# Hash-bucket attention and a gated convolution: two of six transposes per head through DRAM and VectorE

## The chip, the cores and the metric

The kernel runs on one NeuronCore of one Trainium2 chip. The metric is the device time of one execution in microseconds (us); lower is better. The time given for a kernel is the median of its runs. A profile is taken of one execution; its own time is called the span.

Engines are named as in the profile: PE (TensorE), DVE (VectorE), ACT (ScalarE), POOL (GpSimd), and SP, whose queue issues nearly all DMAs here.

## What is computed

The input is attention with 4 batches of 8 heads, 768 rows of 64 numbers, followed by a gated feed-forward block of width 512. Each query and key gets a bucket of 6 sign bits, and a query sees only the keys of its own bucket:

```python
mask = q_bucket[:, :, :, None] == k_bucket[:, :, None, :]
scores = scale * np.matmul(q, k.transpose(0, 1, 3, 2))
scores = np.where(mask, scores, -1000000000.0)
attn = softmax(scores)                       # max, exp, sum + 1e-9
x = (attn @ v)  laid out as (4, 768, 512)
gate = sigmoid(causal_conv(x, conv_w))       # 5 taps, per channel
out = (gate * (x @ w_val)) @ w_out
```

Everything is in 32-bit floats. The three weights arrive as 64-bit floats and are turned into a high and a low part on the chip.

## The kernel before

A head is a unit (32 of them, `units`), and each unit has six tiles of 128 queries (`tiles`, 192 in all). The main loop runs over the slot number k; slot k works on tile k at several stages at once:

- `scores(k + 1)`: four matmuls on PE write the scores of the next tile, 128 x 768, to one of two PSUM buffers `s`. The bucket mask is folded into the matmul by 12 extra rows.
- `maxima(k)`, `factors(k)`, `shifts(k)` on DVE: row maximum `nm`, then the scale `gs` and the shift `nb`. `row_sums` and `recip` do two tiles at once, on even slots.
- `exponentials(k)` on ACT: reads `s`, writes the probabilities `p` (one of four buffers, `LAG + 1`).
- `normalise(k - 2)` on POOL: divides `p` by its row sum.
- `transposes(k - 3)` on PE: six 128 x 128 transposes of `p` into two PSUM tiles `tp` of 384 columns.
- `keep_transposed(k - 4)` on ACT: two copies from `tp` to the buffers `pt`. A head has four `pt` tiles, one for each half of its queries and each half of its keys; there are six buffers.
- `attn_v`: when the sixth tile of a head has been kept, its products with v are put in the list `avs`. They are made on odd slots, two steps a slot, 24 matmul instructions a head, two query halves side by side in one PSUM tile `av`. ACT then copies them to `x`.

Beside it, lists of generators hand out work a step at a time: `preps` (the split of the next head's q and k into high and low parts, with six DMAs between buffers), `convs` (for each pair of heads, the split of `x` into `xh` and `xl`, then the five taps of the gate `g` on POOL and DVE), `moes` (the two products with the weights, in three passes of high and low parts, with the split of the hidden tile into `hh` and `hl`, and the stores of `o`), and `weights` (two chains that load and convert the weight parts in turn, with two staging buffers).

The order of instructions on PE, ACT, DVE and POOL is the order in which the loop writes them down (`manual_schedule`); each engine works through its list strictly in that order. The order of the DMAs on SP is not: a planner sets it when the program is built, and SP then issues them strictly in that order, waiting at each until its data or its buffer is ready. The lines that the prediction steps touch are L266 (scores), L272 (maxima), L282 (shifts), L290 (exponentials), L305 (normalise), L314 (transposes), L323 (copies to `pt`), L337 (`av`), L357 and L408 (the casts to `xh` and `hh`), L368 (the gate's taps), L174 to L182 (the DMAs of `prep`) and L434 (the stores).

Of the kernel before, what the change touches and what calls it, by code (L numbers as in the profile page):

```python
# [26 lines left out]
def kernel(  # L27
# [18 lines left out]
    LAG = 3  # L46
    scale = 1.0 / float(D) ** 0.5
# [9 lines left out]
    ptp = ctx.enter_context(tc.tile_pool(name="ptp", bufs=6))  # L57
# [4 lines left out]
    wst = ctx.enter_context(tc.tile_pool(name="wst", bufs=2))  # L62
# [68 lines left out]
    def load_weights(which):  # L131
        parts = [(src[:, c, :], hl[0][:, c, :], hl[1][:, c, :])
                 for src, hl in ((w_val, wv), (w_out, wo)) for c in range(NP)]
        for src, hi, lo in parts[which::2]:
            if src.dtype == mybir.dt.int64:
                w = wst.tile([P, 512, 2], I32, name="w64")
                nc.sync.dma_start(out=w, in_=src.bitcast(I32).rearrange("p (n t) -> p n t", t=2))
            else:
                w = wst.tile([P, 512], FP32, name="w32")
                nc.sync.dma_start(out=w, in_=src)  # L140
            yield
            yield from split_weight(w, hi, lo)
# [53 lines left out]
    def bits(i):  # L196

        u = stk.tile([P, S], FP32R, name="u", bufs=2)
# [85 lines left out]
    def exponentials(k):  # L284
# [5 lines left out]
        nc.scalar.activation(out=p, in_=s[:, :, 0:HS], func=AF.Exp, bias=nb, scale=gs.pop(k), accum_out=sm[:, k % 2, 0:1])  # L290
# [15 lines left out]

    def transposes(k):
# [9 lines left out]
    def keep_transposed(k):  # L317
        i, qt = tiles[k]
        if qt % 3 == 0:
            cur["pts"].append([ptp.tile([P, 3, HS], FP32, name="pt") for _ in range(2)])  # L320
        qo = (qt % 3) * P
        for pt, tp in zip(cur["pts"][-1], tps.pop(k)):
            nc.scalar.copy(out=pt[:, :, qo:qo + P], in_=tp[:, 0:HS].rearrange("p (a b) -> p a b", b=P))  # L323
        if qt == KB - 1:
            avs.append(attn_v(i, cur["pts"]))
            cur["pts"] = []

    def attn_v(i, pts):
# [4 lines left out]
        for kb in range(KB):  # L333
            if kb:
                yield
            for s, pt in enumerate(pts):
                nc.tensor.matmul(out=av[s * D:(s + 1) * D, 0:HS], lhsT=vt[:, kb, hh * D:(hh + 1) * D], rhs=pt[kb // 3][:, kb % 3, :],  # L337
                                 start=(kb == 0), stop=(kb == KB - 1), tile_position=(0, s * D))
# [11 lines left out]

    def pair_x(b, c, x, gs, xs_):
        for o in (0, HS):
# [4 lines left out]
            nc.vector.tensor_copy(out=xh, in_=x0)  # L357
# [26 lines left out]
    def moe(b, xs_, g):  # L384
# [7 lines left out]
        def val(o, j):  # L392
# [13 lines left out]
            def split():  # L406
                hh = hp.tile([P, HS], FP32R, name="hh")
                nc.vector.tensor_copy(out=hh, in_=ht)  # L408
# [6 lines left out]
        def outp(o, tb):  # L415
            for gens in weights:
                finish(gens)
# [40 lines left out]
    raws, stacks, vts, ss, nbs, ps, tps, sums, rcs, nms, gs, cur = {}, {}, {}, {}, {}, {}, {}, {}, {}, {}, {}, {}  # L458
    avs, convs, moes, early = [], [], [], {}
# [14 lines left out]
    cur["gates"], cur["end"], cur["pts"] = 0, False, []  # L474
    N = len(tiles)
    with tc.manual_schedule(engines=ENGINES):
# [4 lines left out]
        weights = [[load_conv(), load_weights(0)], [load_weights(1)]]  # L481
# [4 lines left out]
        step(weights[0])  # L486
        step(weights[1])
        ahead = [early_bits()]
        turn = 0
        for k in range(N + LAG + 1):  # L490
            if 0 <= k - LAG - 1:
                keep_transposed(k - LAG - 1)
# [9 lines left out]
            if 0 <= k - 2 < N:  # L502
                normalise(k - 2)
            if k < N:
# [24 lines left out]
            if 0 <= k - LAG < N:  # L529
# [68 lines left out]
```

## Time and profile before

| | |
|---|---|
| runs | 621.98, 623.14, 624.74 us; median 623.14 |
| span of the profiled execution | 620.8 us |
| PE busy | 585.5 us, 94% |
| DVE busy | 437.6 us, 70% |
| ACT busy | 421.4 us, 68% |
| POOL busy | 395.6 us, 64% |
| DMA, all queues | 64.64 MB, mean 104 GB/s |

A line of groups of instructions reads: source line, engine, operation, tile written <- tiles read, shapes, count | busy us, mean ns of one | idle time of the engine just before them, and what ended it. A line of the timeline reads: start, duration (both us), engine, line, operation, tiles, count, and in brackets the idle time before it. A line of waits reads: who waited, for whom, us in total, times, longest. Slot times follow from counting: the n-th row maximum (L272) is that of tile n.

### The profile page before, as it was taken

To read this page: it belongs to the slowest core of one execution; us is meant where nothing else is said; L and a number is where in the kernel's file an instruction comes from. 1 tells how busy PE (TensorE), PEld (TensorE's weight loads), DVE (VectorE), ACT (ScalarE), POOL (GpSimd) and SP (SyncE) were. 2 spreads that over 40 slices of the span, in tenths; PEclk is the share of its full clock that TensorE was granted. 3 is DMA by queue.
4 is the path that set the end of the run, shared out by engine and by line. 5 is a ranking of instruction groups with operands and counts; after the bars stand their busy time and mean duration, and the time that the engine had idled before them with its cause. 6 is when DMAs were issued, how large, how long until landed. Compare 5 with 4: busy or idle time off the path is not lost.

```text
span 620.8 us, 10648 instructions
## 1 busy us (share of the span) xinstructions
PE 585.5 (94%) x3496; PEld 423.4 (68%) x3496; DVE 437.6 (70%) x1017; ACT 421.4 (68%) x881; POOL 395.6 (64%) x373
## 2 busy tenths in 40 slices
PE   5789898989999999999999999999999999999997
PEld 2655565555657777776767777777667877775895
DVE  5869798998975866668575867569665877665532
ACT  2777777778778666777787676777787766765400
POOL 3576868778766765578564777568764777544321
PEclk9799999999999999999999999999999999999999
DMA  6467666564532235243433234333422213200111
GB/s 227 123 197 199 200 167 208 157 175 118 133 83 68 70 79 142 72 108 82 122 82 107 61 80 126 84 115 82 108 70 78 67 42 91 69 18 1 51 52 51
DMA packets 29031, 64.64 MB, mean 104 GB/s; under 512 B 4937, under 2 KB 10057, under 8 KB 28977
## 3 DMA queue, kind: packets, MB, share of 16 engines
q1 hardware_dynamic: 28832, 63.93, 37.8%
q8 instruction: 28, 0.46, 0.3%
q14 instruction: 27, 0.21, 0.1%
q10 hardware_dynamic: 144, 0.03, 0.0%
HBM read 30.60 MB, written 7.86 MB: 62 GB/s over the span
## 4 chain that ended last, share of the span: by engine, by line
PE 66%; DVE 12%; ACT 12%; DMA 5%; issue 3%; POOL 2%; SPq 1%; ACTq 0%; POOLq 0%; DVEq 0%
PE av L337 17%; PE s L266 16%; PE tp L314 12%; PE m L424 8%; PE m L399 7%; ACT p L290 5%; DVE nm L272 4%; ACT pt L323 3%; ACT x L345 2%; DMA w<-in_w_val_dram 2%; DVE g L368 2%; PE tp L399 1%; PE tp L424 1%; PE s L424 1%; DMA bk<-bq 1%
## 5 line engine op out<-in xcount | busy, mean ns | idle before, releaser
L305 POOL TENSOR_SCALAR p<-p,ri 128x768 f32<-128x768 f32 x192 | 210.5, 1100 | 156.0 <-DVE nb L282 130.8
L272 DVE TENSOR_REDUCE nm<-s 128x1 f32<-128x768 f32 x192 | 182.5, 950 | 61.2 <-PE s L266 61.0
L290 ACT ACTIVATE p<-s,nb,gs 128x768 f32<-128x768 f32 x192 | 192.6, 1003 | 46.2 <-DVE nb L282 41.9
L323 ACT COPY pt<-tp 128x384 f32<-128x384 f32 x384 | 165.7, 485 | 75.3 <-PE tp L314 74.4
L314 PEld LDWEIGHTS tp<-ident,p 128*128 128x128 f32 x1152 | 130.3, 142 | 72.2 <-issue 43.6
L314 PE MATMUL tp<-ident,p 128*128 128x128 f32 x1152 | 164.4, 279 | 2.6 <-ACT pt L323 2.1
L337 PE MATMUL av<-pt,vt 128*64 128x384 f32 x768 | 144.9, 498 | 0.0
L266 PE MATMUL s<-ak,aq 76*128 76x384 f32 x384 | 118.1, 389 | 23.2 <-ACT p L290 19.7
L266 PE MATMUL s<-bk,bq 128*128 128x384 f32 x384 | 101.3, 345 | 0.4 <-DVE bq L252 0.4
L337 PEld LDWEIGHTS av<-pt,vt 128*64 128x64 f32 x768 | 47.0, 136 | 61.5 <-issue 61.4
L266 PEld LDWEIGHTS s<-ak,aq 76*128 76x128 f32 x384 | 59.2, 194 | 38.7 <-ACT p L290 34.6
L368 DVE SCALAR_TENSOR_TENSOR g<-x,cw_sb,g 128x768 f32<-128x768 f32 x64 | 79.4, 1241 | 2.2 <-POOL g L366 2.1
L266 PEld LDWEIGHTS s<-bk,bq 128*128 128x128 f32 x384 | 71.7, 194 | 0.8 <-issue 0.8
L173 POOL TENSOR_TENSOR bq<-r,aq 128x768 fp32r<-128x768 f32 x31 | 59.2, 1909 | 0.1
L410 POOL TENSOR_TENSOR hl<-ht,hh 128x384 fp32r<-128x384 f32 x32 | 32.3, 1009 | 39.5 <-DVE hh L408 39.5
L345 ACT COPY x<-av 64x384 f32<-64x384 f32 x64 | 30.4, 475 | 29.7 <-PE av L337 29.0
L282 DVE TENSOR_SCALAR nb<-nm,gs 128x1 f32<-128x1 f32 x192 | 40.4, 211 | 3.5
L399 PE MATMUL m<-xh,wv 128*128 128x384 f32 x200 | 42.7, 337 | 0.0
L358 POOL TENSOR_TENSOR xl<-x,xh 128x384 fp32r<-128x384 f32 x32 | 33.4, 1059 | 13.8 <-DVE xh L357 13.8
L290 ACT ACTIVATION_READ_ACCUMULATOR p<-s,nb,gs 128x1 f32 x192 | 39.0, 203 | 0.0
L404 DVE TENSOR_TENSOR ht<-m,g 128x384 f32<-128x384 f32 x25 | 13.9, 556 | 35.6 <-PE m L399 29.2
L424 PE MATMUL m<-wo,hh 128*128 128x512 f32 x144 | 38.1, 394 | 0.0
(86 smaller groups left out, 486.9 us busy)
## 6 DMA issues: line engine op xcount, KB each, us to landing
r<-in_qk_dram SPq DMA_DIRECT2D x32, 384.0 KB
vt<-in_v_dram SPq DMA_DIRECT2D x16, 384.0 KB
out_dram<-o SPq DMA_DIRECT2D x24, 256.0 KB
ak<-aq SPq DMA_DIRECT2D x31, 192.0 KB
bk<-aq SPq DMA_DIRECT2D x31, 192.0 KB
bk<-bq SPq DMA_DIRECT2D x31, 192.0 KB
bq<-aq SPq DMA_DIRECT2D x31, 192.0 KB
hh<-in_qk_dram SPq DMA_DIRECT2D x16, 192.0 KB
```

The source lines that it names most:

```text
L173: nc.gpsimd.tensor_tensor(out=bq, in0=r, in1=aq.bitcast(FP32), op=ALU.subtract)
L266: nc.tensor.matmul(out=s[:, hf, 0:HS], lhsT=lq[0:n, qs], rhs=rk[0:n, hf * HS:(hf + 1) * HS], start=n == M, stop=n == P)
L272: nc.vector.tensor_reduce(out=nm, in_=s[:, :, 0:HS], axis=AX.XY, op=ALU.max, negate=True)
L290: nc.scalar.activation(out=p, in_=s[:, :, 0:HS], func=AF.Exp, bias=nb, scale=gs.pop(k), accum_out=sm[:, k % 2, 0:1])
L305: nc.gpsimd.tensor_scalar(out=p, in0=p, scalar1=rcs.pop(k), scalar2=1.0, op0=ALU.mult, op1=ALU.mult)
L314: nc.tensor.transpose(out=tp[:, n * P:(n + 1) * P], in_=p[:, kb * P:(kb + 1) * P], identity=ident)
L323: nc.scalar.copy(out=pt[:, :, qo:qo + P], in_=tp[:, 0:HS].rearrange("p (a b) -> p a b", b=P))
L337: nc.tensor.matmul(out=av[s * D:(s + 1) * D, 0:HS], lhsT=vt[:, kb, hh * D:(hh + 1) * D], rhs=pt[kb // 3][:, kb % 3, :], start=(kb == 0), s ...
L345: nc.scalar.copy(out=x[hh * D:(hh + 1) * D, o:o + HS], in_=av[s * D:(s + 1) * D, 0:HS])
L368: nc.vector.scalar_tensor_tensor(out=g, in0=x[:, k:k + S], scalar=w, in1=g, op0=ALU.mult, op1=ALU.add)
L399: nc.tensor.matmul(out=acc[:, 0:HS], lhsT=wv[wi][:, c, j * P:(j + 1) * P], rhs=xs_[(c, o)][xi], start=(m == 0), stop=(m == 11))
L424: nc.tensor.matmul(out=acc, lhsT=hs[(o, j)][hi][:, tb * P:(tb + 1) * P], rhs=wo[wi][:, j, :], start=(m == 0), stop=(m == 11))
```

## The change

From tile 60 to tile 185, the first two tiles of each head (`by_blocks`) are no longer transposed on PE. Their `exponentials` write `p` in another order of columns, in blocks of 32. After `normalise`, `put_out` stores `p` to DRAM in one DMA; `take_in`, three slots later in the loop's order, reads it back in four DMAs, one for each quarter of the partitions, which move the 32 x 32 blocks to their places; `turn_blocks`, eight slots after the tile's own slot, transposes each 32 x 32 block in place with one DVE instruction.

The buffers `pt` become four whole half-heads (three query tiles by all keys), with the columns of a tile in the order query block, key tile, key within the block; the copies of `keep_transposed` write that order and `av` reads it, for all heads. `xh` and `hh` are cast by ACT, not DVE, while the slot number is from 60 to 191 (`rounded`). The weights are converted in one chain, with one staging buffer, more steps in a slot, and a wait of two slots between a load and its use. The buffer `u` of the sign bits is one, not two.

```diff
+    QB = 32
+    G = P // QB
+    FIRST, LAST = 60, B * H * KB - KB
...
-    ptp = ctx.enter_context(tc.tile_pool(name="ptp", bufs=6))
+    ptp = ctx.enter_context(tc.tile_pool(name="ptp", bufs=4))
...
-    wst = ctx.enter_context(tc.tile_pool(name="wst", bufs=2))
+    wst = ctx.enter_context(tc.tile_pool(name="wst", bufs=1))
...
+    def load_weights():
+        for src, hl in ((w_val, wv), (w_out, wo)):
+            for c in range(NP):
...
+                since = cur["k"]
+                yield
+                while cur["k"] < since + 2:
+                    yield
+                yield from split_weight(w, hl[0][:, c, :], hl[1][:, c, :])
+                since = cur["k"]
+                while cur["k"] == since:
+                    yield
...
+    def by_blocks(k):
+
+        return FIRST <= k < LAST and k % KB < 2
...
-        u = stk.tile([P, S], FP32R, name="u", bufs=2)
+        u = stk.tile([P, S], FP32R, name="u", bufs=1)
...
-        nc.scalar.activation(out=p, in_=s[:, :, 0:HS], func=AF.Exp, bias=nb, scale=gs.pop(k), accum_out=sm[:, k % 2, 0:1])
+        to, of = p, s[:, :, 0:HS]
+        if by_blocks(k):
+            to = p.rearrange("p a b -> p (a b)").rearrange("p (g a j x) -> p a j g x", g=G, a=2, x=QB)
+            of = of.rearrange("p a (j g x) -> p a j g x", g=G, x=QB)
+        nc.scalar.activation(out=to, in_=of, func=AF.Exp, bias=nb, scale=gs.pop(k), accum_out=sm[:, k % 2, 0:1])
...
+    def put_out(k):
+
+        p, _ = ps.pop(k)
+        pds[k] = dram.tile([P, S], FP32, name="pd")
+        nc.sync.dma_start(out=pds[k], in_=p)
+
+    def take_in(k):
+
+        w = place(k)
+        rows = pds.pop(k).rearrange("(i q) (g c) -> g q i c", q=QB, g=G)
+        for g in range(G):
+            nc.sync.dma_start(out=w[g * QB:(g + 1) * QB].rearrange("q i j x -> q i (j x)"), in_=rows[g])
+
+    def turn_blocks(k):
+
+        w = place(k).rearrange("p i j x -> p (i j x)")
+        nc.vector.transpose(out=w, in_=w)
+        placed(k)
+
+    def place(k):
+
+        i, qt = tiles[k]
+        at = pts.setdefault(i, {})
+        if qt // 3 not in at:
+            at[qt // 3] = ptp.tile([P, 3, G, KB, QB], FP32, name="pt")
+        return at[qt // 3][:, qt % 3]
...
-        for pt, tp in zip(cur["pts"][-1], tps.pop(k)):
-            nc.scalar.copy(out=pt[:, :, qo:qo + P], in_=tp[:, 0:HS].rearrange("p (a b) -> p a b", b=P))
...
+        for a, tp in enumerate(tps.pop(k)):
+            nc.scalar.copy(out=place(k)[:, :, 3 * a:3 * a + 3].rearrange("p i j x -> p j i x"),
+                           in_=tp[:, 0:HS].rearrange("p (j i x) -> p j i x", i=G, x=QB))
+        placed(k)
...
-                nc.tensor.matmul(out=av[s * D:(s + 1) * D, 0:HS], lhsT=vt[:, kb, hh * D:(hh + 1) * D], rhs=pt[kb // 3][:, kb % 3, :],
+                nc.tensor.matmul(out=av[s * D:(s + 1) * D, 0:HS], lhsT=vt[:, kb, hh * D:(hh + 1) * D], rhs=pt[:, :, :, kb, :],
...
+    def rounded(out, in_):
+        if FIRST <= cur["k"] < N:
+            nc.scalar.copy(out=out, in_=in_)
+        else:
+            nc.vector.tensor_copy(out=out, in_=in_)
...
                 normalise(k - 2)
+                if by_blocks(k - 2):
+                    put_out(k - 2)
...
                 exponentials(k)
+            if by_blocks(k - 8):
+                turn_blocks(k - 8)
             if k >= 60 or k % 2:
                 step(convs)
-            for _ in range((1, 0, 2, 0, 2, 2)[k % 6]):
-                step(weights[turn])
-                turn = 1 - turn
+            for _ in range((1, 1, 2, 1, 2, 2)[k % 6]):
+                step(weights)
...
                 step(avs)
+            if by_blocks(k - 5):
+                take_in(k - 5)
-            if 0 <= k - LAG < N:
+            if 0 <= k - LAG < N and not by_blocks(k - LAG):
                 transposes(k - LAG)
```

More of the change, by code (lines that the diff above doesn't have):

```diff
@@ L129, in load_conv @@
             nc.sync.dma_start(out=cw_sb, in_=conv_w)
[L131 to L142, printed above, removed]
+    def load_weights():
+        for src, hl in ((w_val, wv), (w_out, wo)):
+            for c in range(NP):
+                if src.dtype == mybir.dt.int64:
+                    w = wst.tile([P, 512, 2], I32, name="w64")
+                    nc.sync.dma_start(out=w, in_=src[:, c, :].bitcast(I32).rearrange("p (n t) -> p n t", t=2))
+                else:
+                    w = wst.tile([P, 512], FP32, name="w32")
+                    nc.sync.dma_start(out=w, in_=src[:, c, :])
+                since = cur["k"]
[6 more added lines that the diff above has]
+                    yield
     def load_raw(i):
@@ L305, in normalise, with placed @@
         nc.gpsimd.tensor_scalar(out=p, in0=p, scalar1=rcs.pop(k), scalar2=1.0, op0=ALU.mult, op1=ALU.mult)
+    def put_out(k):
[17 more added lines that the diff above has]
+        return at[qt // 3][:, qt % 3]
+    def placed(k):
+        i, _ = tiles[k]
+        done[i] = done.get(i, 0) + 1
+        if done[i] == KB:
+            avs.append(attn_v(i, pts.pop(i)))
     def transposes(k):
@@ L335, in attn_v @@
                 yield
-            for s, pt in enumerate(pts):
-                nc.tensor.matmul(out=av[s * D:(s + 1) * D, 0:HS], lhsT=vt[:, kb, hh * D:(hh + 1) * D], rhs=pt[kb // 3][:, kb % 3, :],
+            for s, pt in sorted(pts.items()):
+                nc.tensor.matmul(out=av[s * D:(s + 1) * D, 0:HS], lhsT=vt[:, kb, hh * D:(hh + 1) * D], rhs=pt[:, :, :, kb, :],
                                  start=(kb == 0), stop=(kb == KB - 1), tile_position=(0, s * D))
@@ L356, in pair_x @@
             x0 = x[:, KW - 1 + o:KW - 1 + o + HS]
-            nc.vector.tensor_copy(out=xh, in_=x0)
+            rounded(out=xh, in_=x0)
             nc.gpsimd.tensor_tensor(out=xl, in0=x0, in1=xh.bitcast(FP32), op=ALU.subtract)
@@ L407, in split @@
                 hh = hp.tile([P, HS], FP32R, name="hh")
-                nc.vector.tensor_copy(out=hh, in_=ht)
+                rounded(out=hh, in_=ht)
                 hl = hp.tile([P, HS], FP32R, name="hl")
@@ L415, in outp @@
         def outp(o, tb):
-            for gens in weights:
-                finish(gens)
+            while weights:
+                cur["k"] += 1
+                step(weights)
             acc = acc_tile()
@@ L472, in finish @@
             step(gens)
-    cur["gates"], cur["end"], cur["pts"] = 0, False, []
+    cur["gates"], cur["end"], cur["k"] = 0, False, 0
     N = len(tiles)
@@ L480 @@
         first_prep()
[L481 removed]
+        weights = [load_weights()]
         preps = [first_bits(), prep(1)]
@@ L485 @@
         step(preps)
-        step(weights[0])
-        step(weights[1])
+        step(weights)
+        weights.insert(0, load_conv())
+        step(weights)
         ahead = [early_bits()]
-        turn = 0
         for k in range(N + LAG + 1):
-            if 0 <= k - LAG - 1:
+            cur["k"] = k
+            if 0 <= k - LAG - 1 and not by_blocks(k - LAG - 1):
                 keep_transposed(k - LAG - 1)
```

10 lines of the change are left out of this document (3 added, 7 removed).

## The prediction

> **What bounds the kernel now.** I read the page's busy line first, then the busy time by stage, then TensorE's own order of time.
>
> ```profile
> span 620.8 us, 10648 instructions
> PE 585.5 (94%) x3496; PEld 423.4 (68%) x3496; DVE 437.6 (70%) x1017; ACT 421.4 (68%) x881; POOL 395.6 (64%) x373
> PE 66%; DVE 12%; ACT 12%; DMA 5%; issue 3%; POOL 2%; SPq 1%; ACTq 0%; POOLq 0%; DVEq 0%
> ...
> 100.00:150.00 50.00, 44.67 (x284) 28.27 (x284) 46.79 (x103) 37.81 (x82) 42.03 (x39) 1.00 0.61 170
> 200.00:250.00 50.00, 49.85 (x301) 37.66 (x300) 33.89 (x80) 34.46 (x75) 33.88 (x33) 1.00 0.38 98
> 350.00:400.00 50.00, 49.92 (x301) 36.96 (x300) 36.81 (x87) 34.69 (x74) 34.46 (x33) 1.00 0.36 94
> ```
>
> The last three rows are stretches of 50 us: busy time of PE, weight load, DVE, ACT and POOL, then granted clock, DMA share, GB/s. Up to about 170 us DVE (46.79 of 50) is as full as TensorE. From 200 us TensorE has no idle time (49.85, 49.92 of 50, clock 1.00) while DVE and ACT have 13 to 16 us of 50 free. The 60th tile's row maximum stands near 173 us and the 192nd's near 561 us, so every tile that the change touches lies in the part where TensorE is full. There a microsecond off TensorE is worth up to a microsecond.
>
> Busy time of matmuls is modelled, so what a transpose costs is read from start to start:
>
> ```profile
> 301.79 1.51 PE L337 MATMUL av<-pt,vt 128*64 128x384 f32 x8
> 303.23 0.88 PE L314 MATMUL tp<-ident,p 128*128 128x128 f32 x6
> 303.86 0.59 PE L266 MATMUL s<-ak,aq 76*128 76x384 f32 x2
> ...
> 305.59 0.82 PE L314 MATMUL tp<-ident,p 128*128 128x128 f32 x6
> 306.24 0.61 PE L266 MATMUL s<-ak,aq 76*128 76x384 f32 x2
> ```
>
> Six transposes hold TensorE 303.86 - 303.23 = 0.63 us and 306.24 - 305.59 = 0.65 us, so 0.64 us a tile.
>
> **The change, part by part.** A slot is one turn of the main loop, one tile. Tiles 0 and 1 of each head from tile 60 to 185 go the new way: 21 heads, 42 tiles.
>
> *Removed.* 42 x 0.64 = **26.9 us of TensorE**. On ACT 84 copies go:
>
> ```profile
> L323 ACT COPY pt<-tp 128x384 f32<-128x384 f32 x384 | 165.7, 485 | 75.3 <-PE tp L314 74.4
> L345 ACT COPY x<-av 64x384 f32<-64x384 f32 x64 | 30.4, 475 | 29.7 <-PE av L337 29.0
> L272 DVE TENSOR_REDUCE nm<-s 128x1 f32<-128x768 f32 x192 | 182.5, 950 | 61.2 <-PE s L266 61.0
> L368 DVE SCALAR_TENSOR_TENSOR g<-x,cw_sb,g 128x768 f32<-128x768 f32 x64 | 79.4, 1241 | 2.2 <-POOL g L366 2.1
> L357 DVE CAST xh<-x 128x384 fp32r<-128x384 f32 x32 | 17.7, 567 | 12.5 <-ACT x L345 10.6
> L408 DVE CAST hh<-ht 128x384 fp32r<-128x384 f32 x32 | 17.6, 550 | 0.3
> L91 ACT ACTIVATE o<-w 128x512 f32<-128x512 f32 x8 | 5.4, 675 | 3.8 <-DMA w<-in_w_val_dram 3.3 <-DMA w<-in_w_out_dram 0.5
> ```
>
> 84 x 0.485 = 40.7 us of ACT go, hidden under TensorE, so 0.
>
> *Rounding moved from DVE to ACT.* By the loop's counts I estimate 22 xh and 24 hh of 32 each. DVE loses 22 x 0.567 + 24 x 0.550 = 25.7 us; ACT gains 46 x 0.475 = 21.9 us (the copy of 384 elements beside it), less than the 40.7 it lost. Cost 0; without the removed copies it would fill 22 of the some 120 free microseconds of ACT in this part.
>
> *Added on DVE.* 42 block transposes of 128x768. No row shows one. [...] I take the 0.95 of the one-source pass over 768 elements. Total 39.9 us, net 14 on DVE over 390 us, with room.
>
> Place matters more than total. A turn is issued after the slot's shift (nb); the second of a head stands in the ninth slot after its tile 0, and that same slot starts the head's av. So the last thing av waits for is no longer an ACT copy at the slot's head, but a DVE pass behind nb:
>
> ```profile
> 203.56 0.21 DVE L282 TENSOR_SCALAR nb<-nm,gs 128x1 f32<-128x1 f32 x1
> 204.78 0.87 PE L337 MATMUL av<-pt,vt 128*64 128x384 f32 x4
> ...
> 481.06 1.27 DVE L357 CAST xh<-x 128x384 fp32r<-128x384 f32 x2
> 484.50 0.21 DVE L282 TENSOR_SCALAR nb<-nm,gs 128x1 f32<-128x1 f32 x1
> 485.05 1.51 PE L337 MATMUL av<-pt,vt 128*64 128x384 f32 x8
> ...
> 555.98 0.21 DVE L282 TENSOR_SCALAR nb<-nm,gs 128x1 f32<-128x1 f32 x1
> 556.53 0.87 PE L337 MATMUL av<-pt,vt 128*64 128x384 f32 x4
> ```
>
> These are the first, the 17th and the last of the 21 heads. nb ends at 203.77 and av starts at 204.78: a turn of 1.0 us with its hand-over just fits. In the last head nb ends at 556.19 and av starts at 556.53: TensorE would wait 0.66 us. Done so for all 21, the waits add to 12.0 us over 14 heads (7.8 in the heads with xh casts just before, such as the 17th, 4.1 in the others). Where the casts go to ACT (1.27 us off DVE in slot eight, 0.95 of turn in their place, and an hh of 0.35 to 1.16 gone too), nb comes about 0.6 us sooner, which leaves some 2.4 of the 7.8. So **+6.5 us**; ends 0 and 21 x 1.0 = 21. While TensorE waits, the next scores and the conv's gates are queued behind av.
>
> The turn also puts off the next tile's row maximum, thus its exponential and the scores two tiles on. In slots with a gate pass (1.24 us, one in three) DVE then has nb, turn, gate and maximum in line, some 3.6 us against slots of 2.5 to 3.5: **+2 us**, ends 0 and 9 (0.45 a head).
>
> *Added: the DRAM trip.* Five DMA issues a tile, 210 in all.
>
> ```profile
> q1 hardware_dynamic: 28832, 63.93, 37.8%
> SPq L182 <- PE s L266: 103.6, 23, 7.8
> SPq L434 <- ACT o L432: 45.1, 5, 34.3
> 337.19 0.46 SPq L176 DMA_DIRECT2D bk<-bq  x1
> 339.87 0.47 SPq L177 DMA_DIRECT2D bq<-aq  x1
> ```
>
> 63.93 MB took 37.8% of 620.8 us, so 272 MB a ms; 42 x 2 x 0.393 = 33.0 MB more is 121 us, which lifts the share in this part from 0.36 to about 0.67. Not a bound. SP's issues cost 210 x 0.46 = 97 us, some 4.6 us a head of 18. Landing: L177 must wait until bk<-bq has landed, so 0.197 MB takes 339.87 - 337.19 = 2.7 us from its issue; 0.197 MB more adds 0.7: **3.4 us** a leg; ends 2.7 and twice that, 5.4, with traffic doubled. The leg back may take 3.4 and three more issues (1.4): with the leg out 8.2 us after the normalisation, against six slots of 2.5 us or more before the turn. It is hidden.
>
> [...] The trace has 2.7 us for half the bytes within SBUF; no run here shows the DRAM leg.
>
> The leg out matters for another reason. Exponentials have four p buffers; tile k+4 takes the one of tile k, now free only when its leg out has landed:
>
> ```profile
> 179.88 2.55 POOL L305 TENSOR_SCALAR p<-p,ri 128x768 f32<-128x768 f32 x2 [0.52 <-DVE nb L282]
> 186.35 1.01 ACT L290 ACTIVATE p<-s,nb,gs 128x768 f32<-128x768 f32 x1
> ...
> 276.28 0.91 POOL L305 TENSOR_SCALAR p<-p,ri 128x768 f32<-128x768 f32 x1
> 278.04 0.32 SPq L182 DMA_DIRECT2D ak<-ud  x1
> 280.18 1.01 ACT L290 ACTIVATE p<-s,nb,gs 128x768 f32<-128x768 f32 x1
> ...
> 533.68 2.56 POOL L305 TENSOR_SCALAR p<-p,ri 128x768 f32<-128x768 f32 x2 [2.10 <-DVE nb L282]
> 541.61 1.01 ACT L290 ACTIVATE p<-s,nb,gs 128x768 f32<-128x768 f32 x1
> ```
>
> First, shortest and last of 42: tiles 60 and 61 are normalised by 182.43 and the exponential of 64 starts at 186.35; tile 91 by 277.19, that of 95 at 280.18 (3.0 us, the shortest); 180 and 181 by 536.24, that of 184 at 541.61. The middle value is 5.0 us. Against 3.4 plus 0.3 for the shorter slots, 7 of 42 fall short, together 2.2 us; four more where an output store stands ahead in SP's queue. **+3 us**, ends 0 and 10. What waits behind that exponential on ACT: the next copies and av's copy, and through the score buffer TensorE.
>
> *Layout.* av now reads its 384 columns as 12 runs of 32, in all 768 matmuls. No matmul of before reads in runs. ACT's copy in three runs (485) against one run (475) is 5 ns a run: ends 0 and 11 x 5 ns x 768 = 42 us. I take 0, since a run is 128 bytes long; the exponential's new runs cost ACT 42 x 22 x 5 ns = 5 us at most, under TensorE. [...]
>
> *Weights.* The same 8 parts, one staging buffer fewer. Counting the steps, the old chains end in slot 56, the new in 53, both before the first val product; a part now has three slots from its release to its use, not two. ACT's waits for these loads are 3.8 us in all: 0, ends -3.8 and +3.8. One u buffer fewer: 3 refills, a slot behind the reads; 0. Half-head buffers: a head's pair comes free two heads later, in time; 0.
>
> **Sum.** 620.8 - 26.9 + 6.5 + 2 + 3 = 605.4 us for the profiled execution. The three runs stand 1.2 to 3.9 us above its span, the median 2.3: **607.7 us**.
>
> **Rivals.**
> *The turn takes the place of the transposes.* If it is the 1.24 us row and xh's going frees nothing, av waits 12.0 + 14 x 0.29 = 16.1 us, the maxima 6: 620.8 - 26.9 + 16.1 + 6 + 3 + 2.3 = 621. For: 14 of 21 heads show less than 1.0 us of room. Against: DVE idles 61.0 us for scores.
>
> *Slower: the leg out is caught behind another DMA on SP.* SP takes its DMAs in one order, set before the run, and stood 103.6 us at L182. That one is released just before the exponential in question (278.04 against 280.18, mostly nearer). If the leg out stands behind it, the exponential of each head's first such tile comes 0.35 + 3.4 us late, of which TensorE has perhaps 1.4 us of other work: 2.3 x 21 = 48, so 620.8 - 26.9 + 11.5 + 48 + 2.3 = 656; it decides from 0.9 us a head on (18 us, more than the rest of the gain). Against: normalising comes before L182's release in every head, 0.9 us at the least. The runs of 32 at their full 42 us (650) end on this side too.
>
> *Nothing comes back.* DVE and SP stay out of the way and ACT's relief helps: 620.8 - 26.9 - 1 + 2.3 = 595.
>
> That the tiles are not taken off TensorE at all cannot be: 252 transposes are not issued.
>
> **How the numbers follow.** Forecast 0.60 (own range 600 to 614), turn in place 0.18 (614 to 622), slower 0.12, nothing back 0.10. The range 596 to 620 leaves out the slower case and half of the edges. This kernel's measurement tells about 0.5%, 3.1 us, from no change: under 620.0 is faster. Forecast, nothing back and half of the turn case: 0.79; same 0.09; slower 0.12.
>
> **What would show it.** Transposes 900, not 1152; their copies 300; a DVE group of 42 near 0.95 us; TensorE waiting at av for it some 6 us. Wrong would be: matmuls of av above 486 ns or more than 0.19 us apart; exponentials waiting for a DMA by tens of us; PE idle above 20 us between 180 and 560; DVE's turns waiting for DMA.

## The result: 12% slower

The changed kernel takes 698.31 us (median of four runs, 696.82 to 700.04) against 622.74 for the kernel before (median of four runs too): a ratio of 1.121, 95% interval 1.119 to 1.124. The forecast was 607.7 us, in a range of 596 to 620. The profiled execution has a span of 698.3 us. First its page: the span, the busy line, the granted clock in 40 slices, and the chain of waits by engine and by line.

```profile
span 698.3 us, 10550 instructions
PE 600.8 (86%) x3244; PEld 414.9 (59%) x3244; DVE 448.7 (64%) x1014; ACT 405.8 (58%) x842; POOL 384.4 (55%) x373
PEclk9889998999999999998999899898889999999999
PE 50%; DVE 17%; DMA 14%; ACT 6%; POOL 5%; SPq 4%; issue 3%; DVEq 0%; ACTq 0%; POOLq 0%
PE av L381 17%; PE s L278 12%; DMA pt<-pd 7%; PE m L475 6%; PE tp L363 6%; DVE nm L284 5%; PE m L449 4%; ACT p L306 3%; DMA bk<-bq 3%; DVE g L418 2%; POOL bq L185 2%; DVE pt L339 2%; SPq L334 2%; POOL p L321 1%; ACT pt L368 1%
```

TensorE has 252 instructions fewer, as planned, and yet is busy for 15 us more. Its share of the chain fell from 66% to 50%; the leg back (`pt<-pd`), a transfer that the prediction had called hidden, now holds 7% of it.

Where the time went is read from busy time by stretch. The bounds are the row maxima of tiles 60, 126 and 186. The columns are the stretch and its length, busy time of PE, PEld, DVE, ACT and POOL with counts, granted clock, DMA share, GB/s. Before:

```profile
0.00:172.70 172.70, 148.09 (x902) 94.94 (x904) 145.32 (x334) 122.82 (x260) 123.09 (x116) 0.98 0.60 171
172.70:367.80 195.10, 191.11 (x1163) 141.28 (x1164) 135.93 (x327) 145.03 (x303) 129.66 (x122) 1.00 0.35 90
367.80:544.20 176.40, 174.95 (x1054) 130.55 (x1053) 120.88 (x292) 129.68 (x274) 117.03 (x110) 1.00 0.33 84
544.20:620.80 76.60, 71.35 (x384) 56.67 (x382) 35.47 (x67) 23.90 (x47) 25.86 (x26) 0.99 0.09 35
```

After:

```profile
0.00:193.60 193.60, 158.52 (x902) 99.02 (x904) 148.09 (x335) 121.95 (x260) 120.30 (x117) 0.93 0.54 153
193.60:420.20 226.60, 193.46 (x1030) 134.44 (x1032) 140.41 (x324) 136.40 (x279) 124.90 (x122) 0.92 0.55 153
420.20:621.70 201.50, 177.34 (x933) 124.66 (x929) 125.34 (x292) 122.06 (x254) 113.00 (x110) 0.92 0.53 150
621.70:698.30 76.60, 71.48 (x384) 56.82 (x384) 34.81 (x65) 25.44 (x51) 26.24 (x26) 0.99 0.12 42
```

Two losses stand apart. **Up to tile 60**, where not one trip has been made, 193.6 - 172.7 = 20.9 us. **Between tiles 60 and 186**, 428.1 - 371.5 = 56.6 us. The tail is the same.

In the middle part TensorE was idle for 5.4 us of 371.5 before, and for 57.3 of 428.1 after: +51.9. Its busy time is 370.8 against 366.1, although 26.9 us of transposes are gone: some 31.6 us of its work are mere slowness, since the granted clock is 0.92 where it was 1.00. So -26.9 + 51.9 + 31.6 = 56.6. The last term can be checked: TensorE was busy for 60.5 us of this part at a clock of 0.50, which is 30.3 us of lost work. The gain was there; waiting and the halved clock each ate more than it.

The groups of the changed kernel name the wait; a row ends with the idle time before the group and its releaser.

```profile
L381 PE MATMUL av<-pt,vt 128*64 128x384 f32 x768 | 167.1, 562 | 48.6 <-DVE pt L339 44.1
L339 DVE STREAM_TRANSPOSE pt<-pt 128x768 f32<-128x768 f32 x42 | 41.1, 978 | 49.0 <-DMA pt<-pd 48.7
```

Its waits, and then those of SyncE's own queue, with total, times and longest:

```profile
DVE pt L339 <- DMA pt<-pd: 48.7, 17, 5.2
PE av L381 <- DVE pt L339: 44.1, 15, 6.2
```

```profile
SPq L188 <- POOL bq L185: 91.3, 31, 7.2
```

VectorE stands at the turn (L339) 48.7 us for the leg back, and TensorE stands at av 44.1 us for the turn.

### One late leg back, followed through

SyncE's queue near 310 us; these are issues of DMAs, several of one kind in one row.

```profile
307.77 0.34 SPq L327 DMA_DIRECT2D pd<-p  x1
308.21 1.88 SPq L334 DMA_DIRECT2D pt<-pd  x4
312.72 0.47 SPq L186 DMA_DIRECT2D ak<-aq  x1
...
314.47 0.60 SPq L334 DMA_DIRECT2D pt<-pd  x1
319.14 0.47 SPq L188 DMA_DIRECT2D bk<-bq  x1
...
321.77 0.47 SPq L189 DMA_DIRECT2D bq<-aq  x1
322.28 1.81 SPq L334 DMA_DIRECT2D pt<-pd  x3
```

At 307.77 the second tile of a head goes out, and the four quarters at 308.21 are the first tile's. The second tile's first quarter goes at 314.47, but its other three come only at 322.28. Between them stands L188, a copy of the next head's preparation, which waits for POOL's subtraction (L185), and L189 behind it. SyncE takes its DMAs in a fixed order, so three quarters that could have gone at 315 stood 7 us behind a copy for the next head, whose first row maximum comes at 333. In 19 of the 21 heads this copy stands between the second tile's leg out and the end of its leg back. Measured over all 21 heads, from the issue of the leg out to the end of the last issue of the leg back: 6.1 us for the first tile (none over 10), 17.3 us for the second (20 of 21 over 10). The row of SyncE above has L188 behind L185 for 91.3 us in all.

What it releases, and how long TensorE had stood:

```profile
324.48 0.99 ACT L306 ACTIVATE p<-s,nb,gs 128x768 f32<-128x768 f32 x1 [0.52 <-DVE nb L294]
326.27 0.98 DVE L339 STREAM_TRANSPOSE pt<-pt 128x768 f32<-128x768 f32 x1 [1.88 <-DMA pt<-pd]
327.17 0.92 DVE L284 TENSOR_REDUCE nm<-s 128x1 f32<-128x768 f32 x1
327.30 2.83 PE L381 MATMUL av<-pt,vt 128*64 128x384 f32 x8 [3.47 <-DVE pt L339]
328.69 0.99 ACT L306 ACTIVATE p<-s,nb,gs 128x768 f32<-128x768 f32 x1 [3.13 <-DVE nb L294]
330.06 1.01 PE L278 MATMUL s<-ak,aq 76*128 76x384 f32 x2
```

The turn stands ahead of the next row maximum on VectorE, so a late leg holds up not av alone but the whole softmax: nm at 327.17, its exponential at 328.69, the next scores at 330.06. TensorE is idle for 3.47 us, and then the eight matmuls of av take 2.83 us where they took 1.51 before. That is the clock:

```profile
318.60:323.80 5.20, 4.53 (x28) 2.83 (x24) 5.16 (x11) 4.77 (x11) 3.58 (x5) 1.00 0.54 155
323.80:327.30 3.50, 0.03 (x2) 0.00 (x1) 1.55 (x5) 1.24 (x3) 1.37 (x2) 0.68 0.88 315
327.30:330.80 3.50, 3.50 (x10) 1.51 (x11) 1.22 (x5) 1.08 (x2) 1.79 (x2) 0.50 0.41 114
```

A gap of 3.5 us, and the clock is granted at 0.50 in the stretch behind it.

### The profile page after: what moved, and what is told of

The parts are those of the page before. It is cut to its first block, busy times and chain, and to the rows that moved or that the text cites. A ratio compares the mean times of both kernels' runs of the same rounds, so it can differ in the third digit from the quotient of the medians.

```text
span 698.3 us, 10550 instructions
## 1 busy us (share of the span) xinstructions
PE 600.8 (86%) x3244; PEld 414.9 (59%) x3244; DVE 448.7 (64%) x1014; ACT 405.8 (58%) x842; POOL 384.4 (55%) x373
## 4 chain that ended last, share of the span: by engine, by line
PE 50%; DVE 17%; DMA 14%; ACT 6%; POOL 5%; SPq 4%; issue 3%; DVEq 0%; ACTq 0%; POOLq 0%
PE av L381 17%; PE s L278 12%; DMA pt<-pd 7%; PE m L475 6%; PE tp L363 6%; DVE nm L284 5%; PE m L449 4%; ACT p L306 3%; DMA bk<-bq 3%; DVE g L418 2%; POOL bq L185 2%; DVE pt L339 2%; SPq L334 2%; POOL p L321 1%; ACT pt L368 1%
## 5 line engine op out<-in xcount | busy, mean ns | idle before, releaser
L321 POOL TENSOR_SCALAR p<-p,ri 128x768 f32<-128x768 f32 x192 | 200.3, 1048 | 200.5 <-DVE nb L294 133.7
L381 PE MATMUL av<-pt,vt 128*64 128x384 f32 x768 | 167.1, 562 | 48.6 <-DVE pt L339 44.1
L368 ACT COPY pt<-tp 128x384 f32<-128x384 f32 x300 | 129.5, 485 | 41.5 <-PE tp L363 40.3
L278 PE MATMUL s<-ak,aq 76*128 76x384 f32 x384 | 123.1, 403 | 35.3 <-ACT p L306 31.3
L363 PEld LDWEIGHTS tp<-ident,p 128*128 128x128 f32 x900 | 103.0, 143 | 61.8 <-issue 37.6
L363 PE MATMUL tp<-ident,p 128*128 128x128 f32 x900 | 130.8, 282 | 3.2 <-ACT pt L368 2.0
L381 PEld LDWEIGHTS av<-pt,vt 128*64 128x64 f32 x768 | 51.7, 149 | 119.5 <-issue 64.4
L278 PEld LDWEIGHTS s<-ak,aq 76*128 76x128 f32 x384 | 64.0, 205 | 73.4 <-ACT p L306 61.3
L278 PE MATMUL s<-bk,bq 128*128 128x384 f32 x384 | 105.0, 356 | 0.4 <-DVE bq L264 0.4
L418 DVE SCALAR_TENSOR_TENSOR g<-x,cw_sb,g 128x768 f32<-128x768 f32 x64 | 76.4, 1194 | 2.3 <-POOL g L416 2.1
L339 DVE STREAM_TRANSPOSE pt<-pt 128x768 f32<-128x768 f32 x42 | 41.1, 978 | 49.0 <-DMA pt<-pd 48.7
L185 POOL TENSOR_TENSOR bq<-r,aq 128x768 fp32r<-128x768 f32 x31 | 58.8, 1898 | 0.1
L389 ACT COPY x<-av 64x384 f32<-64x384 f32 x64 | 30.4, 474 | 32.3 <-PE av L381 31.5
L475 PE MATMUL m<-wo,hh 128*128 128x512 f32 x144 | 38.8, 400 | 0.0
```

Of the source, the lines that this page charges most:

```text
L185: nc.gpsimd.tensor_tensor(out=bq, in0=r, in1=aq.bitcast(FP32), op=ALU.subtract)
L278: nc.tensor.matmul(out=s[:, hf, 0:HS], lhsT=lq[0:n, qs], rhs=rk[0:n, hf * HS:(hf + 1) * HS], start=n == M, stop=n == P)
L321: nc.gpsimd.tensor_scalar(out=p, in0=p, scalar1=rcs.pop(k), scalar2=1.0, op0=ALU.mult, op1=ALU.mult)
L339: nc.vector.transpose(out=w, in_=w)
L363: nc.tensor.transpose(out=tp[:, n * P:(n + 1) * P], in_=p[:, kb * P:(kb + 1) * P], identity=ident)
L368: nc.scalar.copy(out=place(k)[:, :, 3 * a:3 * a + 3].rearrange("p i j x -> p j i x"), in_=tp[:, 0:HS].rearrange("p (j i x) -> p j i x", i= ...
```

## The experiments

All times are set against the kernel before, run on the same chip (622.5 to 623.6 us). The table has the lengths of the parts in the profiled execution, from its row maxima, and for the middle part TensorE's idle time and the time at half clock. It is the measure of all that follows. Each row is one execution, and two runs of one kernel lie up to 6 us apart, so a difference of a few microseconds between two rows is not shown by them alone. "Half clock" is time at a granted clock of 0.50.

| kernel | to tile 60 | 60 to 186 | behind | PE idle, 60 to 186 | half clock, 60 to 186 |
|---|---|---|---|---|---|
| before | 172.7 | 371.5 | 76.6 | 5.4 | 0 |
| changed | 193.6 | 428.1 | 76.6 | 57.3 | 71.6 |
| e1 new weights chain alone | 194.6 | 371.7 | 76.4 | 5.7 | 0 |
| e2 changed, no trips | 196.2 | 375.0 | 76.8 | 6.4 | 0 |
| x1 changed, turn without trip | 195.2 | 373.8 | 76.7 | 20.0 | 17.1 |
| e12 first tile only | 194.1 | 370.8 | 76.7 | 13.2 | 0 |
| e15 second tile only | 196.4 | 385.6 | 76.7 | 22.5 | 6.8 |
| e14 transposes done as well | 194.3 | 430.2 | 76.6 | 47.5 | 41.0 |
| e16 leg back one slot sooner | 193.9 | 411.0 | 76.9 | 46.0 | 47.8 |
| e17 e16, p freed at once | 194.5 | 390.9 | 76.9 | 36.1 | 27.3 |
| e10 SyncE's order by hand | 203.6 | 389.3 | 76.6 | 32.3 | 23.9 |
| e18 e10, p freed at once | 203.4 | 378.7 | 76.8 | 22.2 | 23.9 |

### The two losses parted

**e1**: the kernel before with the new `load_weights` and its step pattern, and nothing else of the change.

> The kernel before with the weights' chain of the changed kernel alone (one staging buffer, two steps of one chain in a slot); all else as before. Theory W, the chain is the cause of the 21 us that the changed kernel has lost by its 60th tile (193.6 against 172.7 us): 640 to 645 us, the 60th row maximum near 193 us, DVE waiting some 15 us for the weights' step on ACT. Theory L, the new order of columns in pt or the single u buffer is the cause: 623 us, the 60th row maximum at 173 us.

644.65 us, ratio 1.035 (1.031 to 1.039). The whole early loss is the weights' chain; behind tile 60 nothing changes.

**e2**: the changed kernel without trips.

```diff
-        return FIRST <= k < LAST and k % KB < 2
+        return False
```

> The changed kernel with no tile by blocks: every tile is transposed by TensorE, and new column order, four half-heads, one u buffer, weights in one chain and rounding on ACT stay. Theory W: the loss stays before tile 60 only, 640 to 645 us, and the stretch from tile 60 to 186 takes some 372 us as before, clock 0.97 or more. If the rounding on ACT or the new order of columns cost something, that stretch is longer than 375 us.

649.28 us, 1.043 (1.038 to 1.047). Buffers, strided reads and the moved rounding together cost 375.0 - 371.5 = 3.5 us of the middle part; the trip and the turn cost 53.

**e5**: e2 with only the leg out, as a copy that nobody reads.

> The changed kernel with every tile transposed by TensorE (as in the run without the trip, 649.3 us), and the leg out alone added: the 42 tiles are also stored to DRAM, read back by no one. The computation is whole. Theory P, the leg out is what costs (the exponential four tiles on waits for the p buffer, SP's queue gets longer): 660 us or more, exponentials waiting for that DMA by 15 us or more. Theory Q, it is the leg back, or the turn: 649 to 653 us.

649.83 us, 1.043 (1.036 to 1.049): the time is e2's, and the middle part takes 376.7 us against 375.0, so 42 stores of 0.39 MB cost no more than some 2 us.

**x1**: the turn without a trip; POOL's normalise writes straight into the place, and the exchange of the blocks between partitions is left out.

> The changed kernel without the trip: POOL's normalisation of the 42 tiles writes straight into their place in the half-head, and VectorE turns them there at the same slots. The exchange of 32x32 blocks between partition quarters is left out, so these tiles hold blocks in wrong places; all other work is there, with none of the 210 DMAs. Theory Q, the DMAs are late: 649.3 - 26.9 and some 8 for the turn's own waits, 628 to 638 us, clock in the later stretch 0.98 or more. Theory D, the turn in VectorE's order ahead of the next maximum, with TensorE's clock halved by each wait, is enough by itself: 670 us or more.

644.56 us, 1.034 (1.022 to 1.047), between what its two theories gave. With no trip at all, taking 26.9 us off TensorE gains 375.0 - 373.8 = 1.2 us of the middle part. Its two executions took 647.46 us, the profiled one, and 641.65; by the medians the gain on e2 is 4.7 us. The rest is given back:

```profile
PE av L384 <- DVE pt L342: 8.5, 6, 2.3
POOL pt L322 <- PE av L384: 8.7, 5, 4.1
```

TensorE is idle for 20.0 us in place of 6.4, and 17.1 us run at half clock. Of the idle time 8.5 us are av's wait for the turn, the first row, and 10.0 us stand behind exponentials (5.3 in e2). The second row belongs to the experiment, not to the change: POOL writes into the place and must wait until the buffer is free, so part of what is given back may not be the turn's.

### Moving the wait about

Three runs tried to lift the turn's wait; in two it was found elsewhere, in the third it grew.

**e4**: the leg back issued by ACT (`nc.scalar.dma_start` in `take_in`), past SyncE's queue.

> The changed kernel with the four DMAs of the leg back issued by ACT in place of SP; the same bytes, the same slots. Theory A, they are late because they stand in SP's queue behind DMAs that wait for POOL and for the leg out: DVE's waits for them fall from 48.7 us to under 10, the stretch from tile 60 to 186 from 428 to 360 to 380 us, the whole to 640 to 655 us. Theory B, the trip itself is slow (two DRAM legs and doubled traffic): the waits stay at 40 us or more and the time within 10 us of 698.

709.71 us, 1.140 (1.131 to 1.149). VectorE's wait for the leg is nearly gone (0.7 us); but an issue of the leg back that has to wait now holds ACT, whose next copy stands behind it. What these issues waited for was not followed up, and the time is above both forecasts:

```profile
ACT pt L368 <- DMA pt<-pd: 52.3, 11, 6.8
```

**e6**: the turn ten slots behind, not eight.

> The changed kernel with the turn ten slots behind its tile in place of eight (some 6 us later); SP's queue is planned anew. Theories A and B both expect the waits of the turn, at most 5.2 us long, to go mostly: under 12 us in all, and 645 to 665 us. If the time stays near 698 the turn's wait is not what costs, but the p buffers or the late DMAs of the next head.

699.41 us, 1.123 (1.118 to 1.129). The turn waits for its leg 4.6 us in place of 48.7; now exponentials stand 35.1 us for the p buffer that a leg out still reads. The load of v waits for the later av on SyncE, and the legs out stand behind that load (2.1 us behind the normalise on average, where it was 1.1).

```profile
ACT p L306 <- DMA pd<-p: 35.1, 14, 5.1
```

```profile
SPq L166 <- PE av L381: 34.2, 9, 5.0
```

**e7**: SyncE too in written order, otherwise the changed kernel.

```diff
-    with tc.manual_schedule(engines=ENGINES):
+    with tc.manual_schedule(engines=ENGINES | {mybir.EngineType.SP}):
```

> The changed kernel with SP's DMAs, too, in the order in which the loop writes them down, not in the planner's. Theory A, the planner's order holds the leg back behind DMAs of the next head: if so, the waits of the turn for DMA fall from 48.7 us to under 15 and the time to 660 us or less. If every order holds something up because SP has one queue for all, it is 690 us or more and the waits move to other DMAs.

842.32 us, 1.351 (1.339 to 1.364), the slowest of all. The load of v is written first in a head's preparation and waits for av of two heads before, which waits for the turn, which waits for a leg back behind that load:

```profile
DVE pt L339 <- DMA pt<-pd: 169.9, 30, 8.2
```

The written order alone was no remedy; what stands ahead of the leg in it decides.

### Is it the trip, or the place on SyncE?

**e10**: SyncE in written order, with the load of v put late and the leg back four slots behind the tile, ahead of the next head's copies.

```diff
-        load_values(i)
         r = raws[i]
...
+            if by_blocks(k - 4):
+                take_in(k - 4)
+            if late and k % KB == 3:
+                load_values(late.pop(0))
...
-            if by_blocks(k - 5):
-                take_in(k - 5)
```

> The changed kernel with SyncE's queue in written order too, in which the take of a tile stands four slots behind its row maximum, behind the turn of that slot and ahead of the next head's preparation, and the load of v's tile is moved to the fourth slot of a head. Theory Q (the trip itself is short; what makes the leg back late is what stands in front of its four issues on SyncE, which the planner of the changed kernel put behind the copies of the next head's stacks): the turn's waits for a DMA fall from 48.7 us to under 15, the stretch from the 60th to the 186th row maximum falls from 428 us to about 375-390 (373.8 with the turn and no trip), the whole to about 645-660. Rival T (the trip's traffic or its own duration): the legs stay as late as before and the whole stays at 690 or above.

669.82 us, 1.076 (1.070 to 1.083): the middle part falls from 428.1 to 389.3 with the same 42 trips, and the turn no longer waits for a DMA. So most of the loss lies in the order on SyncE and not in the trip as such. The total is above the forecast, because this order costs 10 us ahead of tile 60, and because the p buffer is late in its turn:

```profile
ACT p L309 <- DMA pd<-p: 32.1, 12, 4.4
```

**e12** and **e15**: one tile of each head by blocks, `k % KB < 1` and `k % KB == 1`.

> The changed kernel with one tile of each head by blocks in place of two (21 trips in place of 42). Theory Q (the second tile's leg back is the one whose issues stand behind the next head's preparation on SyncE): the stretch from the 60th to the 186th row maximum is about 378-390 us, that is, well below the middle between none (375.0) and two (428.1). Rival T (each trip costs the same): about 400, the middle.

> The changed kernel with only the second tile of each head by blocks (the kernel before it had only the first: 370.8 us from the 60th to the 186th row maximum, against 375.0 with none and 428.1 with both). Theory Q (the second tile's leg back is the late one, because its four issues come behind the next head's preparation on SyncE): this stretch is about 410-430 us, the whole 685-700. Rival N (the cost comes with the second trip per head, whichever it is: traffic, DRAM or p buffers): about 371-380, the whole about 645.

e12: 644.28 us, 1.035 (1.030 to 1.040); e15: 659.29 us, 1.058 (1.054 to 1.062). The first tile alone gains 4.2 us over none (of 21 x 0.64 = 13.4 us of transposes taken away), a middle part of 370.8 us, below the 378 to 390 that were expected; the second alone loses 10.6. Place matters, but e15's forecast of 410 to 430 failed: alone, the second tile's leg back takes 9.4 us, not 17.3. With one trip fewer the planner orders SyncE anew: the copy `bk<-bq` stands ahead of the end of this leg in 8 of 21 heads, in the changed kernel in 19. The losses don't add (-4.2 and +10.6 against +53.1); that each trip delays the other fits this, but which of SyncE's DMAs does it was not parted.

**e16**: one number, the leg back four slots behind (`take_in(k - 4)`), SyncE's order left to its planner.

> The changed kernel with one number changed: the take stands four slots behind its row maximum in place of five, so that the second tile's four issues are given out ahead of the next head's preparation; SyncE's order is the planner's as in the changed kernel. Theory Q: the stretch from the 60th to the 186th row maximum falls from 428 us to about 375-395, the whole to about 645-665, and the turn's waits for a DMA fall well below 48.7 us. If the planner orders SyncE by something else than the place, it stays near 698.

685.29 us, 1.099 (1.095 to 1.104). The second tile's leg back is down to 8.6 us and the turn waits 1.1 us for it. But the middle part falls only to 411.0, short of the forecast of 375 to 395, and again the p buffer takes over. The third row is SyncE's own:

```profile
ACT p L306 <- DMA pd<-p: 33.5, 10, 6.3
PE s L278 <- ACT p L306: 59.1, 47, 5.7
SPq L166 <- PE av L381: 35.0, 9, 5.6
```

SyncE now stands 35.0 us at the load of v, which waits for av (4.3 us in the changed kernel), mostly with the next head's copies right behind it. e10, which puts that load late, has no such row, and TensorE stands idle for exponentials for 19.2 us of the middle part there, in e16 for 35.0. So an early leg back alone gives back 428.1 - 411.0 = 17.1 us; the other 21.7 up to e10 come with the rest of e10's order, which was not parted further.

**e17** and **e18** take that wait away from e16 and from e10: POOL normalises a tile into its place in `pt`, and the leg out reads it there, so that `p` is free at once.

```diff
+        to = place(k).rearrange("p i j x -> p (i j x)") if by_blocks(k) else p
-        nc.gpsimd.tensor_scalar(out=p, in0=p, scalar1=rcs.pop(k), ...
+        nc.gpsimd.tensor_scalar(out=to, in0=p, scalar1=rcs.pop(k), ...
```

> The changed kernel with the take four slots behind, and POOL's normalise of a tile that goes by blocks writes into its place in the buffer of transposed probabilities; the leg out reads it there, and the leg back writes it there. So the p buffer is free when POOL is done, not when the leg out has landed. Theory R (what is left of the loss once the second leg back is early, 411.0 us from the 60th to the 186th row maximum against 370.8-375.0, is the exponentials' wait for a p buffer that a leg out still reads, 33.5 us of waiting, and the halved clock behind it): this stretch is 375-390 us, the whole 645-665. Rival T (the trips' traffic or the two turns in neighbouring slots): it stays at 405-415, the whole at 680-690.

> The kernel with SyncE's queue in written order (389.3 us from the 60th to the 186th row maximum, with 32.1 us of waits of exponentials for a leg out) and the same normalise into place. Theory R: this stretch falls to about 373-382 us, that is, what the turn without any trip takes (373.8), and all of the loss behind tile 60 is found in two waits, the late leg back and the held p buffer. Rival T: it stays at 385-395.

e17: 661.24 us, 1.062 (1.043 to 1.082), the middle part 390.9, 0.9 us above what was expected: 19.4 us of waits for the leg back have returned, and SyncE stands 45.5 us at the load of v, in 8 of 9 cases with issues of a leg back right behind it. e18: 659.84 us, 1.060 (1.053 to 1.067), the middle part 378.7, within 5 us of the turn without any trip. Its two middle stretches carry a DMA share of 0.62 and 0.63, more than the 0.55 and 0.53 of the changed kernel, in less time:

```profile
203.40:406.00 202.60, 188.29 (x1030) 130.53 (x1032) 149.40 (x324) 136.49 (x279) 128.36 (x122) 0.96 0.62 170
406.00:582.10 176.10, 168.19 (x933) 119.41 (x930) 133.56 (x293) 122.26 (x254) 116.82 (x110) 0.98 0.63 174
```

So the middle loss is parted in two steps: 428.1 - 389.3 = 38.8 us go with the order on SyncE (17.1 of them by e16's earlier leg back alone), then 389.3 - 378.7 = 10.6 with p buffers held by legs out. What is left, 7.2 us above the kernel before, is more than e2 and x1 leave without any trip (3.5 and 2.3), but by less than two runs of one kernel can differ. Traffic is not what cost: e18 has the same 42 trips. The gain has not come back with this. The forecast for the middle part was 371.5 - 15.4 = 356.1 us, and most of the 22.6 us that e18 lacks are lacking in x1 too, which has the turn and no trip.

### Does TensorE still set the pace?

**e14**: the changed kernel with the transposes of the 42 tiles done as well, their results read by nobody.

> The changed kernel with TensorE's transposes of the 42 tiles done as well, their results read by nobody (27 us of TensorE's time put back, no copies). Theory I (TensorE is no longer what sets the pace in the changed kernel: its waits and the halved clock behind them are): the whole stays within about 10 us of 698, with TensorE idle for less and the granted clock above 0.93. Rival P (TensorE's own work still sets the pace): 698 + 27 = 725 us.

704.00 us, 1.131 (1.126 to 1.137): 26.9 us of work put back cost 5.7 us. The middle stretches of e14:

```profile
194.30:418.70 224.40, 199.81 (x1160) 144.28 (x1160) 143.21 (x325) 135.93 (x279) 123.84 (x122) 0.95 0.54 153
418.70:624.50 205.80, 182.93 (x1055) 134.41 (x1055) 127.57 (x292) 122.72 (x254) 113.22 (x110) 0.95 0.52 148
```

Busy time rises by 11.9 us only, idle time falls from 57.3 to 47.5, and half clock from 71.6 to 41.0 us: transposes that nobody reads fill gaps, and the clock stays up more of the time. TensorE no longer sets the pace here.

### The early 21 us

In the changed kernel near 41 us (e1 has a pair of the same kind, held for 5.25 us):

```profile
41.05 0.68 ACT L94 ACTIVATE o<-w 128x512 f32<-128x512 f32 x1 [1.64 <-DMA w<-in_w_val_dram]
41.76 0.43 DVE L96 TENSOR_SCALAR o<-o 128x512 f32<-128x512 f32 x1 [4.70 <-ACT o L94]
42.57 0.95 DVE L284 TENSOR_REDUCE nm<-s 128x1 f32<-128x768 f32 x1
45.18 1.01 PE L278 MATMUL s<-ak,aq 76*128 76x384 f32 x2 [2.09 <-ACT p L306]
```

And its waits, of which this one was 5.1 us in the kernel before:

```profile
DVE o L96 <- ACT o L94: 15.0, 5, 4.7
```

Two steps of one chain fall into one slot: ACT's absolute value, which waits for the load, and VectorE's first pass over it. The second stands ahead of the row maximum. VectorE is held for 4.70 us, the scores are late, and the clock is at 0.50 from 45.1 us on. In the old pattern the chains took turns, so that these two fell apart.

**e9**: the changed kernel with a slot between the two.

> The changed kernel with one edit in the weights' conversion: ACT's absolute value and VectorE's step that reads it are never in the same slot. Theory W', it is this pair in one slot that stalls VectorE (five waits, 15.0 us): the waits fall to under 6 us, tile 60 starts near 180 us in place of 193.6, the time is 682 to 690 us. If the loss comes from the loads with one staging buffer, tile 60 stays at 190 us or later.

690.37 us, 1.108 (1.101 to 1.114): this wait falls from 15.0 to 2.1 us, and tile 60 comes at 184.6, 9.0 us sooner, though not at the 180 that were expected.

**e11**: e1 with one step in every slot.

> The kernel before with the new chain of weights alone, but one step of it in every slot where the change does one or two. Theory B (two steps of one chain in one slot put VectorE behind ScalarE's absolute value, or two passes of VectorE ahead of a row maximum; the row maximum comes late and TensorE stands still): the first 60 slots take about 172-180 us in place of 194.6 and the whole is 622-630. Rival S (the one staging buffer, hence the waiting for a load of each piece, is what costs): the first 60 slots stay at 190 or more and the whole at about 640.

634.47 us, 1.019 (1.014 to 1.025): 178.7 us to tile 60, but the part up to tile 126 is then 6.7 us longer (201.7 against 195.0). Between the two forecasts: 10 of 22 us come back.

**c1** and **c2**: one tile per head, and the two old chains, staged in the fourth `pt` buffer, which is then missing ahead of tile 60; c2 has the old rounding too.

> A version that might be level with the kernel before or ahead of it: the first tile of each head by blocks, and the weights converted in the two chains of the kernel before, with their two staging buffers laid in the fourth buffer of the transposed probabilities, which nobody needs before tile 60. From the parts measured: 172.7 us to tile 60 as before, 370.8 from there to the 186th row maximum, 76.7 behind it: a span of 620.2 against 620.8 of the kernel before, so no difference that can be told, or about 622 in time. If the first 60 slots are not back at 173-176, the chains' form was not what cost there.

> The version with one tile per head and the two old chains of weights, and the rounding of x and of the gated values on VectorE for the whole run, as in the kernel before. Without trips, the change's other edits cost 375.0 - 371.5 = 3.5 us between the 60th and the 186th row maximum; if the rounding moved to ScalarE is what costs them, this takes about 617-619 us, faster than the kernel before by some 0.6%; if VectorE with the turn has no room for it, 621 or more.

c1: 636.72 us, 1.021 (1.018 to 1.024); c2: 638.63 us, 1.024 (1.021 to 1.028). The wait behind the absolute value is gone (3.0 us), and the time at half clock ahead of tile 60 is back at the 6.8 us of the kernel before (27.3 in the changed kernel), but tile 60 still comes at 184.7. A new wait stands there, copies for a half-head buffer that av still reads, 19.9 us up to 185 us. Neither the kernel before nor the changed kernel, which has a fourth buffer there, has such a row:

```profile
ACT pt L368 <- PE av L381: 19.9, 8, 2.5
```

So c1 did not put the early part back, and whether the one staging buffer costs anything by itself stays open. Of the 22 us, 9 to 10 are shown to be the doubled steps; the rest was not parted. The rounding is not in it: the middle part is 374.9 us in c1 and 374.0 in c2. No version was faster than the kernel before.

## Why the prediction was wrong

**"Removed: 26.9 us of TensorE."** The transposes went. The step behind it, a microsecond off TensorE is worth up to a microsecond, holds only while nothing else sets the pace; e14 shows that something did, and x1 that the turn even without a trip leaves little of the gain.

**"It is hidden", of the leg back: the step that failed most.** It summed to 8.2 us (two legs and three issues) and compared that with six slots. The leg out was sized well: where SyncE stood waiting for it, 15 times, it had been 2.4 to 6.9 us since its issue, median 3.4, the value taken. What was missing is standing time. For the leg out the prediction asked what stands ahead of it on SyncE; for the leg back it did not, and that leg's way took 17.3 us in the second tile, from the issue of the leg out to the end of the last issue back, where the prediction's own terms, 3.4 and four issues of 0.46, give 5.2. The row of L176 (`bk<-bq`, L188 after) was quoted, for its landing; its own wait for POOL's bq, a row of the view of SyncE's waits that the prediction quoted from, was not:

```profile
SPq L176 <- POOL bq L173: 97.4, 31, 6.7
```

The slower rival had the mechanism, a DMA caught on SyncE, and the wrong leg: legs out left 0.3 us (second tile) to 1.9 us (first) behind the normalise on average.

**Leg out and p buffer, +3 us.** 3.6 us of such waits in the changed kernel: right as far as it went. But it was masked. Once the legs back were early, it was 33 us (e10, e16), and worth 10.6 to 20.1 us of time (e18, e17).

**The turn: 0.95 us, +6.5 for av, +2 for the maxima.** The pass takes 0.978 us. Its place was mis-sized: x1 has 26.9 - 1.2 = 25.7 us given back (22.2 by the medians) where 8.5 were foreseen, though part of it may be the experiment's own. The rival in which the turn takes the place of the transposes, with 0.18, comes nearest to x1. The 8.5 counted waits; it did not count that a gap of TensorE can be paid again at half clock.

**The clock** is in no step. Before, 6.8 us at half clock stood in one spell ahead of tile 60 and 3.1 at the very end; in the changed kernel 102 us in 21 spells, with TensorE busy for 86 of them, so about 40 us of lost work.

**Weights: 0, ends -3.8 and +3.8.** 20.9 us. The step counted slots and the old waits of ACT for loads. It did not look at what two steps in one slot do to a queue in order: the +3.8 bounds the load's delay, not the row maximum behind it.

**Layout of av: 0, up to 42.** Right, though the 0 was a choice that no run of before had shown. Shortest and median matmul in the changed kernel and before:

```profile
L381 PE MATMUL av<-pt,vt x768: 486/486/902, 35.5 to 651.7; 128*64 128x384 f32 x192
```

```profile
L337 PE MATMUL av<-pt,vt x768: 486/486/538, 34.3 to 574.0; 128*64 128x384 f32 x192
```

Runs of 128 bytes cost these matmuls nothing, 486 ns shortest and median in both; the 902 and the mean of 562 ns go with the halved clock (in e12, with no half clock in the middle part, the mean is 511). **Rounding, copies, traffic: 0.** Right (c2, e5, e18); a share of 0.67 was estimated and 0.63 measured in e18.

Of the signs named as wrong in advance, VectorE's turns waiting for DMA and TensorE idle for over 20 us both came; matmuls of av above 486 ns came too, by the clock and not by the layout; exponentials waiting for a DMA by tens of us came only in e6, e10 and e16.

## What to carry to other kernels

A transfer is hidden only if its issue is: for every DMA added to a queue that runs in order, list what stands ahead of it there and what that waits for, not only its own duration; here the second tile's leg back took 17.3 us, in 19 of 21 heads with a copy that waited for POOL ahead of its end. The same holds for a pass put ahead of a row maximum: it passes on its own wait, here 48.7 us in all, to what stands behind it. And where TensorE is nearly full, price a gap of two or three microseconds at well over its length, since the clock can fall behind it: here 51.9 us of new gaps brought another 31.6 us of slowness.

## What the runs showed of the hardware

Gaps of TensorE shorter than the spells behind them can go with a halved clock. The changed kernel has 20 gaps of 1.5 us and more behind its first 10 us, the longest 6.2. In 18 of them, 1.7 to 6.2 us long, or within 2 us behind, a spell at a clock of 0.50 begins; there are 21 spells in all, 11 of them of 3.4 us, 9 of 6.8 and one of 3.2 at the very end. Not every such gap has a spell behind it: the clock stays at 1.00 behind 1.84 us up to 128.6 us in the kernel before, and behind 1.54 us up to 368.4 us in the changed kernel. Nor does a longer gap always have a longer spell: behind the gap of 2.09 us in the early rows above the clock was at half for 6.8 us from 45.1 us on, behind one of 3.44 us up to 307.9 us for 3.4 us.

A block transpose of 128x768 in fp32 takes 978 ns on VectorE (mean of the 42 at L339 of the changed kernel), near the 948 of a reduction over as many elements.

Work that nobody reads can be nearly free, as e14 showed: 252 transposes, 26.9 us of work, cost 5.7 us, with 9.8 us less idle time and 30.6 us less at half clock in the middle part.
